# First mixer tile through ScalarE, w_out's loads behind a gating tile and one raw block behind a bank copy, in a two-layer attention and gated-mixer kernel

## The chip, the cores and the metric

The kernel runs on one core of a Trainium2 chip. The metric is the device time of one execution in microseconds (us). Five engines work beside each other, each through its own list of instructions in order: PE (TensorE, matmuls), DVE (VectorE), ACT (ScalarE), POOL (GpSimd) and SP, which here issues every DMA. Semaphores tie them together.

## The reference

Two layers, each an attention block and a gated mixer block, on x of 2048 rows by 640 columns, in float32:

```
x = x + attention(layernorm(x));  x = x + mixer(layernorm(x))      # twice
attention: 32 heads of 20, four segments of 512 rows; in each a softmax of
    q k^T and a memory read phi(q) M / (phi(q) z), mixed by a gate; then @ wo
mixer:  z  = gelu(x @ w_in)                   # 640 -> 1728
        z1 = z[:, :864];  z2 = layernorm(z[:, 864:])
        g  = w_sp @ z2 + b_sp                 # 2048 x 2048 over the rows
        out = (z1 * g) @ w_out                # 864 -> 640
```

## The kernel before

Precision: a float32 operand is split into a float16 high half (a cast on ACT) and a low half (a subtraction on DVE or POOL); three float16 matmuls stand for one product. A split tile is turned by a transposing DMA from SP. A "tile" of rows is 128 of the 2048, so there are 16.

**Attention** (both layers): a hand-written order of PE's work by pairs of heads. The softmax's exponentials P and Pb are written by ACT, which also makes their high half PH (L1257); the low half PL (L1259) is POOL's, but for the last `TAIL` = 2 head pairs' second half, which DVE does. The output projection (yps, L1018) adds to x (xt, L1024) and stores it; the last four tiles' projection is left to the next stage.

**Mixer input** (function `phase1b`, L318 on): for each tile, x is loaded (L330; L333 where the projection is still due), normalised to xn, split into xnhl and transposed to th (`split_t`, L293 to L295). Then 30 matmuls (zp, L375) with each half of w_in: wi1 first (the z2 half, L388), wi0 after it (z1, L411). The first tile's xn is made by POOL (L359), the other tiles' by DVE (L287). xn and xnhl share a place in SBUF with tiles that the last attention step still uses. z2 is cut into blocks zh, zl for phase 2, z1 goes to DRAM. In layer 0 this stage also prepares w_out and the first row pair of w_sp (class `Rows`): the steps of `Rows.first` are tied one by one to the gelus, among them `scales(0)`, the maxima `am` (L464) of the loaded wr tiles and the powers of two from them.

**Phase 2**: eight row pairs p. The 2048 x 2048 product is done by a Strassen-like scheme with seven products of 24 matmuls a pair (L621, banks ga, gb, gc, gd in PSUM), from blocks wt and sums wts of w_sp; the results are copied out of the banks by ACT (u, L688) and added by DVE (L691), gated with z1 (cz loaded at L626, u at L633), split, transposed (ut, L647) and multiplied with w_out (cyp, L657, the "tail"). While pair p is multiplied, pair q = p + 1 is prepared: raw blocks (`raw`: wn on ACT L478 and DVE L479, transposed L484) named "21", "12", "11", "22", each of two ACT instructions, and sums on POOL (ts, L591) with splits (wts) on ACT L598 and DVE L599.

**What sets the order.** For PE, ACT, DVE and POOL it follows the code's order as a tile scheduler puts it, with `issue_after` and priorities as hints. SP's queue is one list; each DMA waits at least for the one eight issues before it, and a DMA that waits holds those behind it. Split weights are kept in DRAM by layer 0 and loaded from there in layer 1 (L107 and L1341).

Of the kernel before, what the change touches and what calls it, by code (L numbers as in the profile page):

```python
# [20 lines left out]
NT = S // 128  # L21
# [63 lines left out]
class Weight:  # L85
# [11 lines left out]

    def load(self, stage, width=864, tag="wst", late=False):
# [19 lines left out]
        for k in range(self.nk):  # L118
            n = 128 if k < full else rest
            for c in range(0, self.cols, width):  # L120
                w = min(width, self.cols - c)
                if late and len(last) == 2:
                    split()
                    yield
                if tag == "wr":
                    if k == 0:
                        both = stage.tile([128, S], F32, tag=tag, name="wst")
                    st = both[:n, 1024 * (k % 2):1024 * (k % 2) + w]
# [112 lines left out]
def other_scales(g, stage, pool, psum, tag):  # L241
# [18 lines left out]
    yield False  # L260
    parts = pow2_parts(g, pool, psum, tag, g.wam, 3, 4)
# [28 lines left out]
def split_t(g, hl, t, src, low=None):  # L290

    nc = g.nc
    nc.scalar.copy(hl[:, 0], src)  # L293
    g.low = (low or nc.vector).tensor_tensor(hl[:, 1], src, hl[:, 0], ALU.subtract)
    nc.sync.dma_start(t.rearrange("p i k c -> p (i k) c"), hl.rearrange("p i c -> p (i c)"), transpose=True)  # L295
# [15 lines left out]
def phase1b(g, o_d, x, x1_d, z1_d, zh, zl):  # L311

    nc, tc = g.nc, g.tc
    with ExitStack() as ctx:
        pool = lambda n, b, **k: ctx.enter_context(tc.tile_pool(name=n, bufs=b, reuse_waits="tile", **k))
        pe2, pe3, pe1 = pool("be2", 2), pool("be3", 3), pool("be1", 1)
        wp0, px1, p2, px2, p3 = pool("bw0", 1), pool("bx1", 1), pool("b2", 1), pool("bx2", 1), pool("b1", 3)
        pz1, py, pz0 = pool("bz1", 2, space=PSUM), pool("by", 1, space=PSUM), pool("bz0", 1, space=PSUM)  # L318
        g.wi[0].tiles(wp0)
# [19 lines left out]
        def attn_out(t, *a):  # L339
# [15 lines left out]
            if t:  # L355
                layernorm(g, x1, xn, D, 2, XS)
            else:
                mv, rs = layernorm_stats(g, x1, D, 2, XS)
                nc.gpsimd.tensor_scalar(xn, x1, mv[:, 0:1], rs, ALU.subtract, ALU.mult)  # L359
            return xn  # L360

        def xn_t(xn):
            th = pe3.tile([128, 2, KD, 128], F16, tag="th", name="th")
            hl = pe1.tile([128, 2, D], F16, tag="xnhl", name="xnhl")
            split_t(g, hl, th, xn)
# [48 lines left out]
        with tc.high_priority(offset=HP2):  # L414
            a = load(0)
            xn = attn_out(0, *a)
            a = load(ORDER[1])
            th = xn_t(xn)
        for i, t in enumerate(ORDER):
# [8 lines left out]
            th1 = xn_t(xn) if i + 1 < NT else None  # L428
# [15 lines left out]
class Rows:  # L444
# [14 lines left out]
    def scales(self, q):  # L459
        g, nc, sc = self.g, self.g.nc, self.g.wsc  # L460
        am = g.small.tile([128, 2, 2], F32, tag="am", name="am")
        for c in range(2):
            for r in range(2):
                nc.vector.tensor_reduce(am[:, r, c:c + 1], self.ws[q, c][:, r], AX.XY, ALU.max, apply_absolute_value=True)  # L464
        pw = sc[:, 0, q]
# [20 lines left out]
    def first(self, pool):  # L486
# [31 lines left out]
        with at():  # L518
            self.scales(q)
# [16 lines left out]
def phase2(g, b_sp, x1_d, z1_d, zh, zl, out):  # L536
# [3 lines left out]
    with ExitStack() as ctx:  # L540
# [83 lines left out]
        def load_z1(t):  # L624
            z1 = p1.tile([128, FH], F32, tag="z1", name="cz1")
            nc.sync.dma_start(z1, z1_d[t])  # L626
# [55 lines left out]
        for p in range(NP):  # L682
# [38 lines left out]
            if q and p:  # L721
                raw(q, "11")

            close = tail(*ready) if p else lambda: None
            copy(A, 1, left)
            if q:
                raw(q, "22")
            if p + 2 < NP:
                e = rows.load(p + 2)
# [25 lines left out]
            z1 = load_z1(p)  # L755
            if q:
# [4 lines left out]
            ready = turn(p + 8, u[1], *held)  # L761
            if q:
# [103 lines left out]
class Attention:  # L866
# [6 lines left out]
    TAIL = 2  # L873
# [60 lines left out]
    def start(self):  # L934

        g, nc = self.g, self.nc
        for t in self.qk:
            for h in range(2):
                r = slice(64 * h + 60, 64 * h + 64)
                with ExitStack() as ctx:  # L940
                    if g.hold:
                        ctx.enter_context(self.tc.issue_after(g.hold[2].ins))
                    nc.sync.dma_start(t[r], g.qc[r])

    def prep(self, t):
# [21 lines left out]
        def last():  # L967
# [3 lines left out]
            split_t(g, hl, self.xt[s % 2][:, :, :, c], xt, low=nc.gpsimd)  # L971
# [594 lines left out]
```

## Time and profile before

| | |
|---|---|
| median of 3 runs | 2297.23 us (2293.0 to 2298.25) |
| profiled execution | 2293.45 us |
| its span | 2291.7 us, mean granted PE clock 0.982 |
| layer 0: mixer input from | 624.08 us |
| layer 1: mixer input from | 1746.72 us |

The profile gives, for one execution, each instruction's start and duration, the idle time of its engine before it with what ended that (in square brackets), the waits of an engine by line, and for a stretch of time the busy time of every engine with PE's granted clock (1.00 is full speed). Numbers of tiles are left out of the names. The line numbers in the profile are those of the code above.

### The profile page before, as it was taken

The numbers are of one execution on the slowest core, as the hardware profiler recorded it, in microseconds if no ns is written. First come the engines' busy times: TensorE is split into PE (matmuls) and PEld (weight loads), VectorE is DVE, ScalarE is ACT, GpSimd is POOL, SyncE is SP. The second block draws the span as 40 slices with busy tenths as digits, with TensorE's granted clock in tenths as the row PEclk, the third lists the DMA queues.
The fourth block names the chain that finished last, engine by engine and source line by source line (L and its number), as shares of the span: only waits on it lengthen the run. The fifth ranks groups of instructions, "written<-read, shape, count | busy, mean of one in ns | idle before, by whom it ended". The sixth has DMA issues, their size and how long they took to land.

```text
span 2291.7 us, 53099 instructions
## 1 busy us (share of the span) xinstructions
PE 2105.1 (92%) x21322; PEld 1267.3 (55%) x21322; DVE 1598.9 (70%) x2761; ACT 1252.4 (55%) x1637; POOL 1459.3 (64%) x1300
## 2 busy tenths in 40 slices
PE   6888888999699999999988999989997999999998
PEld 3454555666455555555554556666664555455555
DVE  7677788777687757878745777787765664566563
ACT  4577788888644433333314888888873333333331
POOL 2377888999745445456512889999995443465560
PEclk9999899999899999999999999999998999999999
DMA  5565657444666787676555347553454346777853
GB/s 166 160 154 151 152 151 191 111 117 127 174 179 179 193 223 184 145 180 177 140 146 127 101 115 181 125 120 94 122 132 132 85 114 200 181 184 172 187 132 81
DMA packets 538616, 342.80 MB, mean 150 GB/s; under 512 B 413536, under 2 KB 463968, under 8 KB 538112
## 3 DMA queue, kind: packets, MB, share of 16 engines
q1 hardware_dynamic: 538368, 339.40, 57.6%
q8 instruction: 167, 2.74, 0.5%
q14 instruction: 81, 0.66, 0.1%
HBM read 159.19 MB, written 92.55 MB: 110 GB/s over the span
## 4 chain that ended last, share of the span: by engine, by line
PE 49%; DVE 19%; POOL 9%; DMA 8%; ACT 7%; issue 5%; SPq 2%; DVEq 0%; ACTq 0%; POOLq 0%
PE zp L375 11%; PE ga L621 8%; POOL PL L1259 6%; PE cyp L657 4%; PE qps L1045 3%; PE gb L621 3%; PE pv L1287 3%; PE vps L986 2%; DVE mxs L1248 2%; PE mp L1184 2%; PE kps L1045 2%; DVE wts L599 2%; PE gc L621 2%; PE gd L621 2%; ACT PH L1257 2%
## 5 line engine op out<-in xcount | busy, mean ns | idle before, releaser
L1259 POOL TENSOR_TENSOR PL<-P,PH 128x640 f16<-128x640 f32 x380 | 534.1, 1430 | 51.8 <-PE pv L1287 40.9
L1248 DVE TENSOR_REDUCE mxs<-mp 128x2 f32<-128x1024 f32 (+2 forms) x384 | 320.4, 862 | 145.7 <-PE mp L1175 144.1
L1222 ACT ACTIVATE P<-es,sc 128x1024 f32<-128x1024 f32 (+1 forms) x256 | 271.5, 1061 | 97.3 <-PE es L1175 87.3
L375 PEld LDWEIGHTS <-th 128*128 128x128 f16 x1920 | 188.8, 99 | 194.7 <-DMA th<-xnhl 28.1
L591 POOL TENSOR_TENSOR ts<-ts,wt 128x512 f32<-128x512 f32 x196 | 267.9, 1378 | 11.0
L1257 ACT CAST PH<-P 128x1280 f16<-128x1280 f32 x192 | 239.7, 1248 | 1.9 <-ACT P L1222 0.4
L621 PEld LDWEIGHTS <-wts 128*128 128x128 f16 x1536 | 151.1, 98 | 151.6 <-issue 24.9
L621 PE MATMUL ga<-zh,wts 128*128 128x432 f16 x768 | 213.1, 349 | 18.8 <-ACT u L688 18.8
L281 POOL TENSOR_TENSOR lnrs<-lnve,mhalf 128x1 f32<-128x1 f32 x96 | 60.1, 635 | 258.2 <-DVE lnve L280 238.3
L1259 POOL TENSOR_TENSOR PL<-Pb,PH 128x640 f16<-128x640 f32 x124 | 176.2, 1446 | 18.0 <-PE pv L1287 15.8
L591 POOL TENSOR_TENSOR ts<-wt,wt 128x512 f32<-128x512 f16 x28 | 37.0, 1320 | 235.3 <-DMA wt<-wn 235.3
L986 PE MATMUL vps<-wvh,xt 128*128 128x320 f16 x640 | 156.7, 312 | 29.1 <-DVE relu L1077 21.4
L375 PE MATMUL zp<-wi1h,th 128*128 128x432 f16 x640 | 152.0, 353 | 25.6 <-DMA th<-xnhl 25.5
L1287 PE MATMUL pv<-vs,PL 128*128 128x41 f16 x2560 | 157.4, 181 | 12.7 <-POOL PL L1259 8.4
L657 PE MATMUL cyp<-wuh,ut 128*128 128x320 f16 (+1 forms) x896 | 163.6, 299 | 4.3 <-DMA ut<-un 3.4
L621 PEld LDWEIGHTS <-wt 128*128 128x128 f16 x1152 | 112.7, 98 | 96.5
L657 PEld LDWEIGHTS <-ut 128*128 128x128 f16 (+1 forms) x1344 | 131.1, 98 | 59.2 <-DMA ut<-un 5.7
L1184 PEld LDWEIGHTS <-qk 64*128 64x128 f16 (+1 forms) x2048 | 78.5, 94 | 153.6 <-issue 134.7
L1287 PE MATMUL pv<-vs,PH 128*128 128x41 f16 x2560 | 160.0, 182 | 2.0 <-DVE ab L1303 2.0
L375 PE MATMUL zp<-wi0h,th 128*128 128x432 f16 x640 | 148.5, 346 | 3.0 <-ACT z L411 3.0
L1287 PEld LDWEIGHTS <-PL 128*128 128x128 f16 x2560 | 140.4, 96 | 14.8 <-POOL PL L1259 10.2
L688 ACT ACTIVATE u<-ga,bsp,wsc 128x432 f32<-128x432 f32 x64 | 45.4, 710 | 186.7 <-PE ga L621 174.9
(218 smaller groups left out, 5455.8 us busy)
## 6 DMA issues: line engine op xcount, KB each, us to landing
qk<-st SPq DMA_DIRECT2D x256, 120.0 KB
wr<-in_B_w_sp_dram SPq DMA_DIRECT2D x60, 512.0 KB
z<-z SPq DMA_DIRECT2D x32, 432.0 KB
cz<-z SPq DMA_DIRECT2D x32, 432.0 KB
xt<-in_A_x_dram SPq DMA_DIRECT2D x32, 320.0 KB
st<-qhl SPq DMA_DIRECT2D x40, 256.0 KB
st<-khl SPq DMA_DIRECT2D x40, 256.0 KB
x<-x SPq DMA_DIRECT2D x32, 320.0 KB
```

The lines of the kernel that those rows point to most:

```text
L375: nc.tensor.matmul(zp[:, n, :FHH], a[:, k, :], b[:, k, c:c + FHH], start=(k == 0 and j == 0), stop=(k == KD - 1 and j == 2))
L591: nc.gpsimd.tensor_tensor(t, a, t if b == "t" else get(b), ALU.add if op == "+" else ALU.subtract)
L621: nc.tensor.matmul(ps, w[:, a, k % 4, :], z[:, k, j, :], start=start and k == 0 and i == 0, stop=k == NP - 1 and i == 2, skip_group_check= ...
L657: nc.tensor.matmul(yp[:, n, :320], a[:kn[k], k, :], b[:kn[k], k, n * 320:(n + 1) * 320], start=(k == 0 and j == 0), stop=(k == KO - 1 and ...
L986: nc.tensor.matmul(ps, a[:, k, c], b[:, k, n * 320:(n + 1) * 320], start=(i == 0), stop=(i == 14))
L1045: nc.tensor.matmul(ps, a[:, k, c], b[:, k, :], start=(i == 0), stop=(i == 14))
L1184: nc.tensor.matmul(out[:, h, o:o + w], a[r, ac], b[r, bc], start=o == 0, stop=False, skip_group_check=True)
L1222: g.exp = nc.scalar.activation(P, E, AF.Exp, scale=g.esc)
L1248: e = nc.vector.tensor_reduce(mx[:, :, n, j], mp[:, :, o:o + w], AX.X, ALU.max)
L1257: nc.scalar.copy(PH, P[:, h])
L1259: (nc.gpsimd if h == 0 or n < self.N - self.TAIL else nc.vector).tensor_tensor(PL[:, c], P[:, h, c], PH[:, c], ALU.subtract)
L1287: nc.tensor.matmul(pv[:, i, h, :], x[:, c:c + 128], v[:, j, h0 + h, :], start=(j == 0 and x is PH), stop=(j == i and x is PL), skip_group_ ...
```

## The change

Eight edits, in the order of the work:

1. In layer 0's attention one of the weight-scale steps comes one step later (`other_scales`).
2. `TAIL` is 1: the low half PL of the last pair but one goes from DVE to POOL.
3. The first mixer tile: DVE makes the negated mean, ACT subtracts the mean (xn) and scales the high half by 1/sigma (xnhl), DVE makes the low half with both in one operation, and SP transposes; POOL has no part but in 1/sigma's power. The pools are opened in another order, so that xn, xnhl, the x tiles and th's first buffer lie over the key weights, which are dead by then.
4. w_in's first half lies in one tile for both its halves, and its loads in layer 0 are staged through four slots (two wr tiles) in place of two.
5. `Rows.scales(0)` is spread over two gelu steps; what follows comes one gelu later.
6. Phase 2, pair 0: z1's tile is loaded ahead of w_out; eight of w_out's fourteen loads stand behind it, the other six behind the next transpose.
7. Phase 2, pairs 1 to 6: the raw block "11" stands behind the copy of bank A.
8. Start of layer 1: the low halves of tiles 2 and 3 are DVE's, and the twelve constant loads (qc) stand behind tile 3's transpose.

Its core:

```diff
-        pe2, pe3, pe1 = pool("be2", 2), pool("be3", 3), pool("be1", 1)
+        pe2, pe1, pe3 = pool("be2", 2), pool("be1", 1), pool("be3", 3)
...
-            else:
-                mv, rs = layernorm_stats(g, x1, D, 2, XS)
-                nc.gpsimd.tensor_scalar(xn, x1, mv[:, 0:1], rs, ALU.subtract, ALU.mult)
-            return xn
+                return xn, None
+            mv, rs = layernorm_stats(g, x1, D, 2, XS)
+            neg = g.small.tile([128, 1], F32, tag="neg", name="neg")
+            nc.vector.tensor_scalar(neg, mv[:, 0:1], -1.0, None, ALU.mult)
+            nc.scalar.activation(xn, x1, AF.Identity, bias=neg)
+            return xn, rs
...
+                nc.scalar.activation(hl[:, 0], xn, AF.Identity, scale=rs)
+                nc.vector.scalar_tensor_tensor(hl[:, 1], xn, rs, hl[:, 0], ALU.mult, ALU.subtract)
+                nc.sync.dma_start(th.rearrange("p i k c -> p (i k) c"), hl.rearrange("p i c -> p (i c)"), transpose=True)
...
-        with at():
-            self.scales(q)
+        parts = self.scale_parts(q)
+        for _ in range(2):
+            with at():
+                next(parts, None)
...
             product(A, p, 2, False)
-            if q and p:
-                raw(q, "11")
...
             copy(A, 1, left)
+            if q and p:
+                raw(q, "11")
...
-            if p == 0:
-                with tc.issue_after(e.ins):
-                    for _ in g.wu.load(None):
-                        pass
...
             z1 = load_z1(p)
+            if p == 0:
+                wu = g.wu.load(None)
+                with tc.issue_after(g.z1.ins):
+                    for _ in range(4):
+                        next(wu)
...
             ready = turn(p + 8, u[1], *held)
+            if p == 0:
+                with tc.issue_after(g.hold[2].ins):
+                    for _ in wu:
+                        pass
...
-    TAIL = 2
+    TAIL = 1
...
-                        ctx.enter_context(self.tc.issue_after(g.hold[2].ins))
+                        ctx.enter_context(self.tc.issue_after(self.fourth.ins))
...
+            e = split_t(g, hl, self.xt[s % 2][:, :, :, c], xt, low=nc.vector if g.hold and t in (2, 3) else nc.gpsimd)
```

Three places in the order of instructions. First SP's queue at the start of layer 1's mixer, before (L295 is tile 0's transpose, L107 loads w_in, L1026 stores x):

```order
L333 DMA xt<-x_0_12 128x640
L1026 DMA x_1_11<-xt 128x640
L107 DMA wi0h<-w_i0h 128x864
L107 DMA wi0l<-w_i0l 128x864
L107 DMA wi0h<-w_i0h 128x864
L107 DMA wi0l<-w_i0l 128x864
L107 DMA wi0h<-w_i0h 128x864
L107 DMA wi0l<-w_i0l 128x864
L107 DMA wi0h<-w_i0h 128x864
L107 DMA wi0l<-w_i0l 128x864
L107 DMA wi0h<-w_i0h 128x864
L107 DMA wi0l<-w_i0l 128x864
```

Tile 0's transpose is the next row, behind all ten. The same place now (L1053 stores x, L377 is tile 0's transpose, L111 loads w_in):

```order
L1053 DMA x_1_10<-xt 128x640
L377 DMA_TRANSPOSE th<-xnhl 128x10x128
L1053 DMA x_1_11<-xt 128x640
L111 DMA wi_27858<-w_i0h 128x864
L111 DMA wi_27858<-w_i0l 128x864
L111 DMA wi_27858<-w_i0h 128x864
L111 DMA wi_27858<-w_i0l 128x864
```

The transpose moved ahead of the ten loads, of a store and of the xt load. In layer 0 it stands between the xt load (L338 now, L333 before) and the store of x_0_11.

Second SP's queue in phase 2's pair 0 of layer 0, before (wuh and wul are w_out, cz is z1's tile, ut the transpose):

```order
L107 DMA wuh<-w_uh 128x640
L107 DMA wul<-w_ul 128x640
L107 DMA wuh<-w_uh 96x640
L107 DMA wul<-w_ul 96x640
L626 DMA cz_13890<-z_0_0 128x864
L647 DMA_TRANSPOSE ut<-un 128x14x128
L626 DMA cz_14146<-z_0_9 128x864
L647 DMA_TRANSPOSE ut<-un 128x14x128
```

And now:

```order
L468 DMA wr<-in_B_w_sp_dram 128x2x512 x4
L646 DMA cz_13878<-z_0_0 128x864
L111 DMA wuh<-w_uh 128x640
L111 DMA wul<-w_ul 128x640
L111 DMA wuh<-w_uh 128x640
L111 DMA wul<-w_ul 128x640
L111 DMA wuh<-w_uh 128x640
```

z1's tile moved from behind fourteen loads of w_out to ahead of them.

Third ACT's list in phase 2, one pair p of layer 0, before (u are the copies of bank A, wn the raw blocks, wts the casts of sums):

```order
L688 ACTIVATE u<-ga,bsp,wsc 128x432
L478 ACTIVATE wn<-wr,wsc 128x512 x6
L688 ACTIVATE u<-ga,bsp,wsc 128x432
L478 ACTIVATE wn<-wr,wsc 128x512 x2
L598 CAST wts_16208<-ts_15816 128x512
```

And now:

```order
L708 ACTIVATE u<-ga,bsp,wsc 128x432
L496 ACTIVATE wn<-wr,wsc 128x512 x4
L708 ACTIVATE u<-ga,bsp,wsc 128x432
L496 ACTIVATE wn<-wr,wsc 128x512 x4
L618 CAST wts_16210<-ts_15818 128x512
```

Two of the eight raw instructions moved behind the second copy.

More of the change, by code (lines that the diff above doesn't have):

```diff
@@ L96, in tiles, with paired @@
         return self.h, self.l
+    def paired(self, pool):
+        t = pool.tile([128, self.nk, 2, self.cols], F16, tag=f"w{self.nm}", name=f"w{self.nm}")
+        self.h, self.l = t[:, :, 0], t[:, :, 1]
     def load(self, stage, width=864, tag="wst", late=False):
@@ L126, in load @@
                     if k == 0:
-                        both = stage.tile([128, S], F32, tag=tag, name="wst")
-                    st = both[:n, 1024 * (k % 2):1024 * (k % 2) + w]
+                        four = [stage.tile([128, S], F32, tag=tag, name="wst") for _ in range(2)]
+                    st = four[k // 2 % 2][:n, 1024 * (k % 2):1024 * (k % 2) + w]
                 else:
@@ L260, in other_scales @@
     yield False
+    yield False
     parts = pow2_parts(g, pool, psum, tag, g.wam, 3, 4)
@@ L294, in split_t @@
     g.low = (low or nc.vector).tensor_tensor(hl[:, 1], src, hl[:, 0], ALU.subtract)
-    nc.sync.dma_start(t.rearrange("p i k c -> p (i k) c"), hl.rearrange("p i c -> p (i c)"), transpose=True)
+    return nc.sync.dma_start(t.rearrange("p i k c -> p (i k) c"), hl.rearrange("p i c -> p (i c)"), transpose=True)
 def split_psum(g, h, l, ps, mult=1.0):
@@ L417, in phase1b @@
             a = load(ORDER[1])
-            th = xn_t(xn)
+            th = xn_t(*xn)
         for i, t in enumerate(ORDER):
@@ L427, in phase1b @@
                 a = load(ORDER[i + 2])
-            th1 = xn_t(xn) if i + 1 < NT else None
+            th1 = xn_t(*xn) if i + 1 < NT else None
             if i > 0:
@@ L459, in scales, with scale_parts @@
     def scales(self, q):
+        for _ in self.scale_parts(q):
+            pass
+    def scale_parts(self, q):
         g, nc, sc = self.g, self.g.nc, self.g.wsc
@@ L464, in scales @@
                 nc.vector.tensor_reduce(am[:, r, c:c + 1], self.ws[q, c][:, r], AX.XY, ALU.max, apply_absolute_value=True)
+            if not c:
+                yield
         pw = sc[:, 0, q]
@@ L720, in phase2 @@
             product(A, p, 2, False)
+            close = tail(*ready) if p else lambda: None
+            copy(A, 1, left)
             if q and p:
                 raw(q, "11")
-            close = tail(*ready) if p else lambda: None
-            copy(A, 1, left)
             if q:
@@ L728, in phase2 @@
             if p + 2 < NP:
-                e = rows.load(p + 2)
-            if p == 0:
-                with tc.issue_after(e.ins):
-                    for _ in g.wu.load(None):
-                        pass
+                rows.load(p + 2)
             if p and q:
@@ L970, in last @@
             hl = self.e2.tile([128, 2, D], F16, tag="xh", name="xnhl")
-            split_t(g, hl, self.xt[s % 2][:, :, :, c], xt, low=nc.gpsimd)
+            e = split_t(g, hl, self.xt[s % 2][:, :, :, c], xt, low=nc.vector if g.hold and t in (2, 3) else nc.gpsimd)
+            if t == 3:
+                self.fourth = e
         return stats, norm
```

11 lines of the change are left out of this document (7 added, 4 removed).

## Prediction

> **What bounds the kernel now.** I read the page first: TensorE (PE) is busy for 92% of the span, so time can only come out of the remaining 8%, or out of matmuls that run at a lower clock. Then the list of waits of PE from 620 us to the end of layer 1 (what it waits for; us in total, times, longest).
>
> ```profile
> PE 2105.1 (92%) x21322; PEld 1267.3 (55%) x21322; DVE 1598.9 (70%) x2761; ACT 1252.4 (55%) x1637; POOL 1459.3 (64%) x1300
> PE zp L375 <- DMA th<-xnhl: 25.5, 6, 11.2
> PE ga L621 <- ACT u L688: 18.8, 10, 4.2
> ```
>
> The mixer's first matmuls (zp) wait 25.5 us for the transposed th, and phase 2's matmuls (ga) wait 18.8 us for an ACT copy (u) that frees their PSUM bank. Those are the places that the change touches, so I read the timeline around each. Layer 0's mixer start, with the queue of SP and the granted clock of the stretch behind it:
>
> ```profile
> 611.57 0.34 SPq L333 DMA_DIRECT2D xt<-in_A_x_dram  x1
> 613.53 2.51 POOL L359 TENSOR_SCALAR xn<-x,lnmv,lnrs 128x640 f32<-128x640 f32 x1 [5.81 <-PE yps L1018]
> ...
> 616.07 0.73 ACT L293 CAST xnhl<-xn 128x640 f16<-128x640 f32 x1 [8.73 <-POOL xn L359]
> 617.71 1.12 DVE L294 TENSOR_TENSOR xnhl<-xn,xnhl 128x640 f16<-128x640 f32 x1
> 618.86 2.28 SPq L295 DMA_TRANSPOSE th<-xnhl  x1
> 624.08 0.90 PE L375 MATMUL zp<-wi1h,th 128*128 128x432 f16 x2 [9.63 <-DMA th<-xnhl]
> ...
> 624.08:629.00 4.92, 4.92 (x14) 2.09 (x15) 1.95 (x2) 3.02 (x3) 0.00 (x0) 0.50 0.91 234
> ```
>
> PE stops at 624.08 - 9.63 = 614.45. POOL can only normalise x at 613.53, because xn lies over a buffer that the last output projection (yps) reads; then the split, the transpose issue at 618.86 and 5.2 us to landing. After the pause, 4.92 us run at clock 0.50: 4.92 x 0.50 = 2.5 us more. Layer 1 repeats it, with ten loads of w_in's half ahead of the transpose in SP's queue:
>
> ```profile
> 1729.78 0.33 SPq L1026 DMA_DIRECT2D x<-xt  x1
> 1734.97 0.43 SPq L107 DMA_DIRECT2D wi0h<-w_i0h  x1
> ...
> 1740.88 1.90 SPq L295 DMA_TRANSPOSE th<-xnhl  x1
> 1746.72 0.90 PE L375 MATMUL zp<-wi1h,th 128*128 128x432 f16 x2 [11.21 <-DMA th<-xnhl]
> 1746.72:1752.00 5.28, 5.28 (x15) 2.24 (x16) 0.83 (x1) 2.01 (x2) 0.00 (x0) 0.50 0.88 225
> ```
>
> The pause is 11.21 us, the half clock 5.28 x 0.50 = 2.6 us. Later in layer 0's mixer there is one more pause of note; the busy times of two stretches of 20 us (PE, PE's weight loads, DVE, ACT, POOL, then clock) and two rows of the timeline:
>
> ```profile
> 640.00:660.00 20.00, 19.16 (x109) 10.31 (x108) 18.62 (x36) 10.80 (x19) 9.77 (x10) 1.00 0.69 162
> ...
> 680.00:700.00 20.00, 16.98 (x99) 9.48 (x97) 15.97 (x28) 6.86 (x11) 9.86 (x10) 1.00 0.90 263
> ...
> 685.04 1.22 DVE L464 TENSOR_REDUCE am<-wr 128x1 f32<-128x1024 f32 x1 [2.47 <-DMA wr<-in_B_w_sp_dram]
> ...
> 695.08 0.53 PE L375 MATMUL zp<-wi0h,th 128*128 128x432 f16 x2 [3.02 <-ACT z L411]
> ```
>
> This pause of 3.02 us leaves the clock of its stretch at 1.00. At full clock a matmul of zp takes 19.16 / 109 = 0.18 us, 30 of them 5.3 us.
>
> The sum below is made against the profiled execution (2293.45 us: span 2291.7 and 1.75 around it). The median of the three runs is 3.78 us above it; I take the same gains off the median.
>
> **Part 1, the first mixer tile (xn, xnhl, th of tile 0).** The change puts xn and xnhl over the key weights, which nothing reads any more by then, and takes POOL out. In return ACT does two activations of 128x640, 0.73 us each by its cast of that size. DVE does a small operation and one like the 1.12 us subtraction. They stand in the last third of the attention, beside PE's work, and ACT is busy for 55% of the span: 0, or 2 us a layer if a score waits behind them. So the transpose is bound by its place in SP's queue alone. *Layer 0:* it stands directly behind the xt load, which waits for the last readers of Pb (611.57 + 0.34 = 611.9). With the 5.2 us from issue to landing of the row above it lands at 617.1, and PE pauses 617.1 - 614.45 = 2.7 us. The pause of 3.02 us above left the clock at 1.00, so I count no half clock. Gain 9.63 + 2.5 - 2.7 = 9.4; bounds 6 (the xt load 3 us later, for its readers' sake) and 12.1 (no pause). *Layer 1:* there it stands behind the store at 1729.78, ahead of the ten loads; it lands by 1730.1 + 5.8 = 1735.9, and PE stops at 1746.72 - 11.21 = 1735.5. That is 0.4 us. What is late next is the tenth load, issued as before near 1741 and wanted in order by the second 30 matmuls, from 1735.9 + 5.3 = 1741.2, and tile 8's transpose behind them; I leave 1 us for these. Gain 11.21 + 2.6 - 1.4 = 12.4; bounds 9 and 13.8.
>
> **Part 2, the low halves of the last head pairs (TAIL).** One pair's PL moves from DVE to POOL in each layer.
>
> ```profile
> 600.81 8.33 DVE L1259 TENSOR_TENSOR PL<-P,PH 128x640 f16<-128x640 f32 x2
> 609.86 1.56 DVE L1259 TENSOR_TENSOR PL<-Pb,PH 128x640 f16<-128x640 f32 x2 [0.25 <-PE pv L1287]
> ...
> 600.94 2.75 POOL L1259 TENSOR_TENSOR PL<-P,PH 128x640 f16<-128x640 f32 x2
> ...
> 608.47 0.19 PE L1287 MATMUL pv<-vs,PL 128*128 128x41 f16 x1 [3.02 <-DVE PL L1259]
> ```
>
> Beside POOL's casts the DVE pair took 8.33 us, and PE waited 3.02 us for it; on POOL it would cost 2.75. But the Pb pair that stays on DVE took 1.56 only because POOL was through by then; POOL's row of casts is now 2.75 longer, and if the two overlap, Pb may take what the P pair took, 6.8 us more. I take 0, between a gain of 3 and a loss of 4 a layer, since the row that goes and the row that threatens are of one kind. The Trainium skill ("SBUF — State Buffer", on the two separate sides) says that a DVE operation with two SBUF inputs and a GpSimd operation exclude each other for whole instructions. By turns the pair would take 2 x (0.78 + 1.38) = 4.3 us; this trace's 8.33 is beyond that, so the rows decide.
>
> **Part 3, inside layer 0's mixer.** The weight scales take two steps in place of one. DVE stands 2.47 us for a load in front of the maxima (am), and PE stops 3.02 us for what follows. With half the maxima a step later, DVE passes on. But DVE is busy 18.62 of 20 us a little earlier, and everything is one gelu later: I take 1 (0 to 3). One scale step later in layer 0's attention, wi's paired tile and the four staging slots move small operations in stages where PE runs on; their cover is PE's work there; 0, or 1 us each way if the cover goes.
>
> **Part 4, phase 2's first pair.** SP issues four loads of w_sp (wr) until 852.0, then fourteen of w_out, and only then z1's tile (cz), which the gate's product u waits for:
>
> ```profile
> 849.47 2.55 SPq L456 DMA_DIRECT2D wr<-in_B_w_sp_dram  x4
> ...
> 863.60 0.37 SPq L626 DMA_DIRECT2D cz<-z  x1
> 868.58 1.56 DVE L633 TENSOR_TENSOR u<-u,cz 128x864 f32<-128x864 f32 x1 [3.96 <-DMA cz<-z]
> ...
> 875.09 0.52 PE L621 MATMUL ga<-zh,wts 128*128 128x432 f16 x1 [3.53 <-ACT u L688]
> 875.09:879.00 3.91, 3.91 (x13) 1.71 (x13) 3.91 (x5) 0.00 (x0) 0.00 (x0) 0.58 0.61 117
> 1984.32 1.06 DVE L633 TENSOR_TENSOR u<-u,cz 128x864 f32<-128x864 f32 x1 [4.70 <-DMA cz<-z]
> ...
> 1990.34 0.34 PE L621 MATMUL ga<-zh,wts 128*128 128x432 f16 x1 [4.15 <-ACT u L688]
> ```
>
> Behind the wr loads, cz issues near 852 and has until 868.58 - 3.96 = 864.6, when DVE is free. That is 12 us for a transfer that took 868.5 - 863.6 = 4.9, with the four wr loads ahead of it. DVE starts 3.96 us earlier, which covers the 3.53 us of PE, and the half clock's 3.91 x 0.42 = 1.6 goes with it: 5.2. Layer 1: 4.15 and a like 1.6, covered by 4.70 of DVE: 5.6, taking off 0.2. The six w_out loads that now stand behind the ut transpose issue in 6 x (863.60 - 852.0) / 14 = 5 us, until some 870, and are first read by the w_out tail behind those 24 ga matmuls, which end about 5 us after 871.6. Bounds 2 and 5.8 each: cz may still come late behind wr.
>
> **Part 5, the third raw block behind the bank copy, pairs 1 to 6.** ACT copies bank A (u) behind six raw halves (wn), of which the fifth waits for a transpose. The wait list of 880 to 1125 and ACT's rows in pair 1; then pair 3 of layer 1:
>
> ```profile
> PE ga L621 <- ACT u L688: 9.5, 6, 1.7
> 885.88 0.72 ACT L478 ACTIVATE wn<-wr,wsc 128x512 f16<-128x512 f32 x1 [2.34 <-DMA wt<-wn]
> ...
> 887.91 0.69 ACT L688 ACTIVATE u<-ga,bsp,wsc 128x432 f32<-128x432 f32 x1
> ...
> 2077.44 0.72 ACT L478 ACTIVATE wn<-wr,wsc 128x512 f16<-128x512 f32 x1 [2.29 <-DMA wt<-wn]
> ...
> 2080.75 0.71 ACT L688 ACTIVATE u<-ga,bsp,wsc 128x432 f32<-128x432 f32 x1 [1.21 <-PE ga L621]
> ...
> 2083.08 1.45 POOL L591 TENSOR_TENSOR ts<-wt,wt 128x512 f32<-128x512 f16 x1 [15.28 <-DMA wt<-wn]
> ```
>
> In layer 0 u would start with the fourth wn's end, 885.88 - 2.34 = 883.5, in place of 887.91; the six waits (9.5 us) go. The wn behind it starts at 885.88 as before, since the transpose sets it. I take 8 of 9.5: PE then runs closer on the later sums, whose slack no row shows; bounds 4 and 9.5. In layer 1 u waits for PE until 2080.75 and the raw halves queue behind it: they come some 3.3 us later (2080.75 against 2077.44), and so may POOL's sums. No wait of PE stands there now, so that cost is 0 unless the slack is under 3.3 (rival D).
>
> **Part 6, between the layers.** Twelve constant loads (qc) stand ahead of tile 2's transpose:
>
> ```profile
> 1181.87 9.97 SPq L943 DMA_DIRECT2D qk<-qc  x12
> ...
> 1187.16 2.76 POOL L294 TENSOR_TENSOR xnhl<-xt,xnhl 128x640 f16<-128x640 f32 x2 [0.80 <-ACT xnhl L293]
> 1192.38 3.07 SPq L295 DMA_TRANSPOSE xt<-xnhl  x2
> ...
> 1196.02 0.45 PE L986 MATMUL vps<-wvh,xt 128*128 128x320 f16 x1 [4.16 <-DMA xt<-xnhl]
> ```
>
> Without them the transpose goes with the split's end, 1188 to 1189.9 (DVE's 1.12 against POOL's 1.38 apiece), at least 2.5 us sooner, and two transposes are no longer issued in one go. 4.16 is at stake, and 1.6 if a half clock follows it as after the 3.53; I leave 1.2 for the key weights' load that still fills the queues: 4.6, bounds 2 and 5.8. The qc loads are wanted only by the scores, after all of vps.
>
> **The sum.** 9.4 + 12.4 + 0 + 1 + 5.2 + 5.6 + 8 + 4.6 = 46.2 us: 2297.2 - 46.2 = 2251.0 (2247.2 on the profiled execution's scale). About 0.2%, 4.6 us, is what a measurement of this kernel can tell from none.
>
> **The rivals.**
> *A, given back in the mixer (0.15).* DVE at 18.62 of 20 us becomes the bound of layer 0's mixer once it starts earlier, so that part 1's 9.4 comes back as waits before 700: 2260. For it: DVE's row; against: in that same stretch PE lost only 0.84 us.
> *B, phase 2 keeps its wait (0.12).* cz lands late behind the wr loads, and pairs 1 to 6 meet the next late sum: 5.2 + 5.6 + 4 are lost: 2266.
> *C, the change does not do what it says (0.05).* The transposes stand earlier in SP's queue but issue no earlier, because the queue itself stands, as for 9.97 us at the twelve qc loads: 9.4 + 12.4 are lost: 2273.
> *R, the port rule on TAIL (0.10).* DVE's Pb pair runs beside POOL's longer row and takes 8.33 in place of 1.56; less the 3.02 us of PE that go, that is 3.8 us later at each layer's end: 2251 + 7.6 = 2259. For it: the 8.33; against: POOL's casts took 2.75 beside it, so the overlap may be short. The Trainium skill's page named in part 2 has the rule by which the two exclude each other.
> *D, slower (0.04).* The raw block behind the copy makes every later sum late. Price: 3.3 us and the 2.29 wait inside it, 5.6 in each of 12 pairs, 67 us, and part 5's 8 is not had: 2251 + 75 = 2326. It decides from the point where the slack in layer 1 is under 3.3 us, and wins over the gains when it is under some 1.5.
>
> **How the numbers follow.** The forecast has 0.54, with its own range 2243 to 2259 (its terms' bounds do not all fall to one side). A, R and B lie up to 2266. The range 2240 to 2270 leaves out C, D and the forecast's far ends. Faster by over 0.2%: all but D and a heap of small losses, 0.93; same 0.03; slower 0.04.
>
> **What would show it.** Right: zp's first wait under 4 us in layer 0 and under 2 in layer 1, both at clock near 1.0; no wait of ga on u in pair 1; ga's waits on u in pairs 1 to 6 gone; vps on xt under 1.5. Wrong: new waits of ga or gb on wts in layer 1's pairs (D), waits of zp on z before 700 (A), pv waiting for DVE's PL (R).

## The result and the profile after

The changed kernel takes 2277.91 us (median of 4 runs, 2274.11 to 2279.61) against 2295.11 us (4 runs, 2291.43 to 2298.25) for the kernel before on the same chip: a ratio of 0.9923, with a 95% interval of 0.9901 to 0.9945. That is a gain of some 17 us where 46 were forecast. The profiled executions (2279.19 and 2293.45 us) differ by 14.3 us. The page of the changed kernel shows PE as the busiest engine still, and no other engine near it:

```profile
PE 2107.4 (93%) x21322; PEld 1266.8 (56%) x21322; DVE 1606.0 (71%) x2761; ACT 1250.7 (55%) x1639; POOL 1458.3 (64%) x1300
```

So a loss must stand in waits of PE or in its clock. The first step is a ledger: the same matmul is looked up in both traces at each seam between the stages, and the distances are compared. In the table pv is the attention's last matmul, zp the mixer's first, gb and gd the first of those banks in phase 2's pairs 0 and 7, cyp the last of w_out's tail; us from one to the next.

| stretch | before | after | change | forecast |
|---|---|---|---|---|
| layer 0: start to last pv | 614.3 | 618.2 | +4.0 | 0 |
| last pv to first zp | 9.8 | 2.0 | -7.8 | -6.9 |
| first zp to gb of pair 0 | 225.4 | 236.3 | **+10.8** | -3.5 |
| gb of pair 0 to gd of pair 7 | 285.7 | 272.3 | -13.4 | -13.2 |
| gd of pair 7 to last cyp | 47.2 | 53.7 | **+6.5** | 0 |
| layer 1: last cyp to last pv | 552.9 | 554.2 | +1.3 | -4.6 |
| last pv to first zp | 11.4 | 0.0 | -11.4 | -10.8 |
| first zp to gb of pair 0 | 217.4 | 218.7 | +1.2 | -1.6 |
| gb of pair 0 to gd of pair 7 | 276.0 | 270.9 | -5.1 | -5.6 |
| gd of pair 7 to the end | 51.6 | 51.2 | -0.4 | 0 |

The four large gains came as forecast, within 1 us each (-37.7 against -36.5 in sum). The losses are in stretches that the forecast held to be neutral or better, above all the two in bold. The list of PE's waits from 0 to 2290 us (what it waits for; us in total, times, longest) names what is new there:

```profile
PE ga L641 <- ACT u L708: 11.2, 9, 3.8
...
PE yps L1045 <- DVE xt L1051: 8.5, 2, 5.4
PE zp L387 <- DMA th<-xnhl: 7.6, 7, 2.0
PE zp L387 <- ACT z L423: 5.7, 1, 5.7
...
PE gc L641 <- DMA wt<-w: 2.8, 1, 2.8
```

The wait for th fell from 25.5 to 7.6 us and that for u from 18.8 to 11.2. But yps waits 8.5 us for DVE's residual sum xt, and gc 2.8 us for a transfer; neither wait was there before. Each is followed to its cause in the timeline.

**The end of layer 0's attention** (DVE, POOL, PE and SP from 603 to 621 us):

```profile
603.35 2.75 POOL L1286 TENSOR_TENSOR PL<-P,PH 128x640 f16<-128x640 f32 x2
603.40 9.77 DVE L292 TENSOR_SCALAR xn<-x,lnmv,lnrs 128x640 f32<-128x640 f32 x1 [0.32 <-POOL lnrs L286]
...
606.94 2.75 POOL L1286 TENSOR_TENSOR PL<-P,PH 128x640 f16<-128x640 f32 x2
609.65 2.75 POOL L1286 TENSOR_TENSOR PL<-Pb,PH 128x640 f16<-128x640 f32 x2
612.35 0.47 POOL L1334 TENSOR_TENSOR gm<-ab 128x160 f32<-128x160 f32 x1
613.09 0.54 DVE L1051 SCALAR_TENSOR_TENSOR xt<-yps,sc,xt 128x320 f32<-128x320 f32 x1
613.68 0.42 PE L1045 MATMUL yps<-woh,o 128*128 128x320 f16 x1 [3.08 <-DVE xt L1051]
620.22 0.54 PE L387 MATMUL zp<-wi1h,th 128*128 128x432 f16 x1 [1.81 <-DMA th<-xnhl]
```

Tile 8 is the mixer's second. Its normalisation (xn, L292) writes one of the tiles that the change put over the key weights, so it no longer waits for the attention's buffers and DVE takes it early, among the attention's own work. There it stands for 9.77 us, until 613.17, 0.35 us after the last operation of POOL's row, and the residual sum xt queues behind it. In the kernel before it came only after the attention:

```profile
618.87 0.64 DVE L287 TENSOR_SCALAR xn<-x,lnmv,lnrs 128x640 f32<-128x640 f32 x1
```

How long such an operation takes otherwise in the changed kernel, the group of that line shows (count; shortest, median and longest in ns):

```profile
L292 DVE TENSOR_SCALAR xn<-x,lnmv,lnrs x30: 606/612/10396, 603.4 to 1909.9; 128x640 f32<-128x640 f32 x30
```

The median is 0.61 us; the 10396 is the same instruction in layer 1. There PE's yps waits 5.45 us:

```profile
1716.96 10.40 DVE L292 TENSOR_SCALAR xn<-x,lnmv,lnrs 128x640 f32<-128x640 f32 x1 [1.69 <-POOL lnrs L286]
...
1727.87 0.42 PE L1045 MATMUL yps<-woh,o 128*128 128x320 f16 x1 [5.45 <-DVE xt L1051]
```

What these waits cost on balance is less than their length in layer 0, since another wait went from the same place: the 3.02 us of pv for DVE's PL. Set side by side matmul by matmul, the last pv comes 3.96 us later than before, but 2.39 us of that are already there at the pv that ran at 599.0 us before (now at 601.4). The end of layer 0's attention thus costs 1.6 us. In layer 1 the same reckoning, from the pv at 1708.0 us on, gives 4.2 us.

**Layer 0's mixer.** The pause of zp near 690 us has grown from 3.02 to 5.67 us, and phase 2 now starts with a wait of gc. The matmul after the pause, then SP's issue of the first row pair's blocks and the matmul that waits for them:

```profile
693.58 0.52 PE L387 MATMUL zp<-wi,th 128*128 128x432 f16 x1 [5.67 <-ACT z L423]
...
815.62 4.37 SPq L599 DMA_DIRECT2D wt<-w  x6
...
823.08 0.36 PE L641 MATMUL gc<-zh,wt 128*128 128x432 f16 x1 [2.85 <-DMA wt<-w]
```

Half-speed stretches follow some of the pauses (window, its length, then busy us of PE, its weight loads, DVE, ACT and POOL; granted clock, DMA share, GB/s): behind layer 0's first zp, the wait of ga near 845, layer 1's first zp (where the clock is full), the last row pair of layer 0 (told below) and the long pause. In the trace's clock records the clock is either 0.50 or 1.00; a value between them is a window that holds some of both.

```profile
620.22:624.00 3.78, 3.78 (x12) 1.69 (x13) 3.78 (x4) 3.20 (x5) 1.56 (x2) 0.55 0.42 120
845.08:849.00 3.92, 3.92 (x13) 1.68 (x13) 2.00 (x3) 1.17 (x2) 0.00 (x0) 0.56 0.35 66
1736.75:1740.70 3.95, 3.95 (x28) 2.15 (x25) 1.60 (x4) 0.72 (x1) 1.76 (x3) 1.00 0.78 253
1137.16:1142.43 5.27, 5.27 (x15) 2.17 (x15) 0.65 (x2) 0.00 (x0) 0.00 (x0) 0.50 0.01 3
693.58:698.69 5.11, 5.11 (x15) 2.19 (x15) 4.86 (x6) 2.12 (x4) 3.20 (x3) 0.50 0.73 227
```

The excess of the third stretch of the ledger is then made up of +2.65 (the longer pause), +2.6 (5.11 x 0.50 behind it), +2.85 (gc), +3.2 (ga: 4.0 us in two waits in place of 0.8 in one) and +1.7 (3.92 x 0.44 behind the longer of them), less 1.7 (later waits for th: 3.0 in place of 4.7) and 0.8 (the first zp's half clock, 3.78 x 0.45 = 1.7 in place of 2.5): 10.5 of the 10.8.

**The last row pair of layer 0**, ACT and PE (before, the same three rows stood at 1137.78, 1138.30 and 1139.60 with no such wait in the list):

```profile
1135.88 0.62 ACT L618 CAST wts<-ts 128x512 f16<-128x512 f32 x1 [2.51 <-POOL ts L611]
1136.41 0.70 ACT L708 ACTIVATE u<-ga,bsp,wsc 128x432 f32<-128x432 f32 x1
1137.16 0.52 PE L641 MATMUL ga<-zh,wts 128*128 128x432 f16 x1 [3.79 <-ACT u L708]
```

PE comes to this pair 6.4 us earlier than before, the chain from POOL's sum through ACT's cast to the bank copy u only 1.9 us earlier (1136.41 against 1138.30). PE waits 3.79 us, and 5.27 us at clock 0.50 cost 2.6 more: together the whole lead of 6.4 us.

These traces suggest three causes: **S**, the extra gelu step fetches phase 2's first row pair too late; **L**, in layer 0's last pair ACT's cast of the fourth sum (s4) stands ahead of the bank copy; **X**, tile 8's xn stands beside POOL's row. The rivals: DVE is the bound of layer 0's mixer and gives the gains back there (A of the prediction); and **T**, that w_in's four staging slots pack its splits ahead of tile 8's and delay the early mixer.

### The profile page after: what moved, and what is told of

Read it like the earlier page. It is cut to its first block, busy times and chain, and to the rows that moved or that the text cites. A ratio compares the mean times of both kernels' runs of the same rounds, so it can differ in the third digit from the quotient of the medians.

```text
span 2277.5 us, 53085 instructions
## 1 busy us (share of the span) xinstructions
PE 2107.4 (93%) x21322; PEld 1266.8 (56%) x21322; DVE 1606.0 (71%) x2761; ACT 1250.7 (55%) x1639; POOL 1458.3 (64%) x1300
## 4 chain that ended last, share of the span: by engine, by line
PE 48%; DVE 16%; POOL 10%; DMA 9%; ACT 8%; issue 6%; SPq 2%; ACTq 0%; DVEq 0%; POOLq 0%
PE zp L387 9%; PE ga L641 9%; POOL PL L1286 6%; PE cyp L677 5%; PE qps L1072 3%; PE pv L1314 3%; PE vps L1013 3%; PE mp L1211 2%; PE kps L1072 2%; PE gb L641 2%; DVE mxs L1275 2%; PE gc L641 2%; ACT PH L1284 2%; PE gd L641 2%; PE es L1211 1%
## 5 line engine op out<-in xcount | busy, mean ns | idle before, releaser
L387 PEld LDWEIGHTS <-th 128*128 128x128 f16 x1920 | 188.1, 98 | 179.7 <-DMA th<-xnhl 11.4
L611 POOL TENSOR_TENSOR ts<-ts,wt 128x512 f32<-128x512 f32 x196 | 280.1, 1440 | 11.1 <-DMA wt<-wn 0.2
L641 PE MATMUL ga<-zh,wts 128*128 128x432 f16 x768 | 214.1, 351 | 11.3 <-ACT u L708 11.2
L387 PE MATMUL zp<-wi,th 128*128 128x432 f16 x960 | 183.7, 350 | 5.7 <-ACT z L423 5.7
L1211 PE MATMUL es<-qk 64*128 64x512 f16 (+3 forms) x1024 | 124.8, 300 | 24.6 <-ACT P L1249 20.0
L1314 PEld LDWEIGHTS <-PL 128*128 128x128 f16 x2560 | 140.7, 97 | 11.5 <-POOL PL L1286 11.4
```

Source lines behind the costliest of these rows:

```text
L387: nc.tensor.matmul(zp[:, n, :FHH], a[:, k, :], b[:, k, c:c + FHH], start=(k == 0 and j == 0), stop=(k == KD - 1 and j == 2))
L611: nc.gpsimd.tensor_tensor(t, a, t if b == "t" else get(b), ALU.add if op == "+" else ALU.subtract)
L641: nc.tensor.matmul(ps, w[:, a, k % 4, :], z[:, k, j, :], start=start and k == 0 and i == 0, stop=k == NP - 1 and i == 2, skip_group_check= ...
L1211: nc.tensor.matmul(out[:, h, o:o + w], a[r, ac], b[r, bc], start=o == 0, stop=False, skip_group_check=True)
L1314: nc.tensor.matmul(pv[:, i, h, :], x[:, c:c + 128], v[:, j, h0 + h, :], start=(j == 0 and x is PH), stop=(j == i and x is PL), skip_group_ ...
```

## The experiments

Ten runs follow, on three chips. Each ratio holds against runs of the kernel before on the same chip (medians 2289.67, 2294.21 and 2292.8 us). The changed kernel was run again on the second chip alone (ratio 0.9917 [0.99, 0.9933]), so a ratio from the first or third is set beside the changed kernel's only through the kernel before. A stretch of the ledger is named by its two ends, as in the table above.

### The scales in one step again (S)

```diff
-        parts = self.scale_parts(q)
-        for _ in range(2):
-            with at():
-                next(parts, None)
+        with at():
+            self.scales(q)
```

> The changed kernel with the weight scales of layer 0's mixer in one step again. Theory S (the fourteenth step puts the last loads of the first row pair one gelu later, and that is what makes phase 2 of layer 0 start late): the wait of gc for the block wt (2.85 us) and the wait of ga for the bias load (3.2 us, with 1.7 us of half clock behind it) go; phase 2's first pair starts some 6 to 8 us earlier, and the pause of zp near 693 (5.67 us) stays within 2 us of itself. Theory D (DVE and the loads of w_sp bound that stage whatever the steps): the pause near 693 stays or grows and phase 2's first pair starts within 2 us of where it does now. Time against the changed kernel: S 5 to 8 us less, D within 2 us.

Measured: 2269.55 us, ratio 0.9905 [0.9878, 0.9932]. PE's waits from 815 to 850 us, of the changed kernel and of this one:

```profile
PE ga L641 <- ACT u L708: 3.2, 1, 3.2
PE gc L641 <- DMA wt<-w: 2.8, 1, 2.8
```

```profile
PE ga L639 <- ACT u L706: 1.4, 2, 0.8
```

The wait of gc is gone with the step, so S holds: the step delayed the fetch of the first blocks by one gelu and PE stood for it. From the first zp to pair 0's gb this run takes 228.7 us, where the changed kernel took 236.3 (232.8 in a second execution) and the kernel before 225.4. In the total the gain of 5 to 8 us that was expected is not shown, since the interval overlaps the changed kernel's. The pause near 690 only fell to 4.90 us, so the step is not its main cause.

### The last pair's cast behind the bank copy (L)

```diff
-                if not q:
-                    split(p, "s4")
...
-            if p and q:
+            if p:
                 split(p, "s4")
```

> The changed kernel with the last pair's split of s4 behind the copy of bank A, as in the pairs before it. Theory L (layer 0's last pair pays back what the pairs before gained, because the copy of bank A stands behind casts of POOL's last sum): the wait of ga on u near 1137 (3.79 us) and the half clock behind it (3.84 us at 0.50) go, 5 to 6 us less, and layer 1's phase 2 stays as it is. Rival (POOL's sums are late as such, and the wait only moves to the next product that reads s4): the wait reappears as one of ga on wts some 9 us later, under 2 us less.

Measured: 2268.57 us, ratio 0.9904 [0.9883, 0.9925]. PE's waits from 870 to 1150 us, which in the changed kernel hold the one of 3.8 us:

```profile
PE ga L641 <- ACT u L708: 1.9, 4, 0.8
```

The longest is 0.8 us, and no wait of ga stands later in the pair either. From gd of pair 7 to the last cyp this run takes 47.1 us, against 53.7 in the changed kernel and 47.2 before: L holds, and the 6.5 us are shown at their place. In the total they are not, since the intervals overlap.

### Tile 8 centred on ACT too (X)

Tile 8's xn goes the way of the first tile, over ACT, and so out of DVE's queue.

```diff
-            if t:
+            if t and t != ORDER[1]:
                 layernorm(g, x1, xn, D, 2, XS)
```

> The changed kernel with tile 8, the second of the mixer, centred and scaled on ACT like the first. Theory B (DVE's normalisation of tile 8, which now comes early, took 9.8 and 10.4 us because it can't run while POOL's casts follow one another, and the residual sum xt behind it kept the projection waiting): the waits of yps on xt of 3.08 us (layer 0) and 5.45 us (layer 1) go; 6 to 8 us less if they are not eaten by the stage behind, of which layer 1's 4 to 5 should stay in the total and layer 0's may be eaten. Rival (PL casts left on DVE are the cause): the waits stay within 1 us, no change in the total.

Measured: 2270.1 us, ratio 0.9915 [0.9889, 0.9941]. The waits of yps on xt are gone in both layers. PE's waits from 600 to 620 us show what is late next:

```profile
PE pv L1314 <- DVE ab L1330: 2.9, 1, 2.9
...
PE zp L387 <- DMA th<-xnhl: 1.8, 1, 1.8
```

The same row of 2.9 us stands in layer 1. So DVE's xn did hold xt back, but in layer 0 3.08 us of wait turned into 2.9 of another, and in layer 1 5.45 into 2.9. Matched matmul by matmul as above, the ends of the two attentions now cost 0.3 and 1.9 us against the kernel before, in place of 1.6 and 4.2. The total cannot be told from the changed kernel's.

### TAIL back at 2, the control for X

If DVE's xn waits out POOL's row, it must get shorter by exactly what is taken out of that row: the two PL operations of one pair, 2.75 us.

```diff
-    TAIL = 1
+    TAIL = 2
```

> The changed kernel with TAIL 2: the last pair but one's second low half on DVE again. Theory B (POOL's unbroken row of casts blocks DVE's normalisation): POOL's row is two casts shorter, but DVE gets its pair of 5 to 8 us back; the waits at the end of both attentions stay between 2 and 6 us a layer; total within 4 us. Rival (moving the pair to POOL is what made DVE late): the waits of yps on xt fall under 1 us in both layers and the total falls by 4 to 8 us.

Measured: 2276.36 us, ratio 0.9936 [0.9913, 0.9959]: no gain over the changed kernel. DVE's two rows, layer 0 and layer 1:

```profile
601.09 7.06 DVE L292 TENSOR_SCALAR xn<-x,lnmv,lnrs 128x640 f32<-128x640 f32 x1 [0.32 <-POOL lnrs L286]
...
1714.16 7.69 DVE L292 TENSOR_SCALAR xn<-x,lnmv,lnrs 128x640 f32<-128x640 f32 x1 [1.69 <-POOL lnrs L286]
```

9.77 - 7.06 and 10.40 - 7.69 are both 2.71 us: the row's two operations of PL. Here too xn ends 0.35 us after the last operation of POOL's row. Its time is POOL's row and not its own work. That is shown; the price in total is not. In layer 0 the wait of yps is gone, but pv waits 3.4 us for DVE's PL, and in layer 1 yps still waits 2.7 us and zp again 3.9 us for th.

### The changed kernel once more

> The changed kernel itself once more, on the chip of the three runs beside it, to have them compared on one chip. All theories: the ratio against the kernel before between 0.990 and 0.9945, as measured.

Measured: 2272.55 us, ratio 0.9917 [0.99, 0.9933], a gain of 21.7 us on this chip. Its profiled execution tells which of the new waits belong to the kernel. The first zp and PE's waits from 815 to 850 us:

```profile
618.14:622.10 3.96, 3.96 (x22) 2.16 (x23) 3.96 (x4) 3.81 (x5) 1.66 (x3) 1.00 0.38 110
```

```profile
PE gc L641 <- DMA wt<-w: 3.5, 1, 3.5
PE ga L641 <- ACT u L708: 1.3, 2, 0.8
```

The waits of yps (3.1 and 5.4), gc (3.5), the last pair (3.62) and the pause near 690 (5.87) are all there again. The wait of 3.2 us of ga near 845 and the half clock at the first zp (its pause was 1.2 us here and not 1.81) are not. Pair 0's gb comes at 850.94, 232.8 us after the first zp in place of 236.3, so 3.5 of the 10.8 us come and go between executions (the wait of ga near 845 stands in X's run again, 3.1 us long). Matched as above, the ends of the two attentions cost 2.2 and 4.2 us here, while at 599 us only 0.3 us had been lost, not 2.39.

### The kernel before with the raw block moved (part 5 alone)

```diff
             product(A, p, 2, False)
-            if q and p:
-                raw(q, "11")
 
             close = tail(*ready) if p else lambda: None
             copy(A, 1, left)
+            if q and p:
+                raw(q, "11")
```

> The kernel before with one part of the change alone: raw block 11 behind the copy of bank A. Theory L: the six waits of ga on u in pairs 1 to 6 of layer 0 (9.5 us) shrink to under 2, but the last pair, whose s4 cast stands ahead of its bank copy, pays 3 to 6 us of it back as one wait of ga on u near 1130 (with half clock); net gain 3 to 6 us; layer 1 unchanged within 1 us. Rival D of the prediction (the later raw block makes POOL's sums late in every pair): waits of ga or gb on wts in layer 1's pairs, no gain or a loss.

Measured (10 runs): 2289.88 us, ratio 0.9982 [0.9968, 0.9997], that is 0.7 to 7.3 us. PE's waits from 880 to 1160 us:

```profile
PE ga L621 <- ACT u L688: 5.4, 4, 3.7
```

The six waits of 9.5 us of the kernel before have become four of 5.4, of which 3.7 us is one wait, at 1134.5 in the last pair: the numbers of the changed kernel (5.4, 4 times, longest 3.8). In layer 1's pairs PE's list is empty, so rival D's late sums did not come. Part 5 alone gains 9.5 - 1.7 = 7.8 us in pairs 1 to 6, as forecast, and in the same breath makes the last pair's wait of 3.7 us: from gd of pair 7 to the last cyp this run takes 53.7 us, as the changed kernel does.

### Two staging slots again (T)

```diff
-                        four = [stage.tile([128, S], F32, tag=tag, name="wst") for _ in range(2)]
-                    st = four[k // 2 % 2][:n, 1024 * (k % 2):1024 * (k % 2) + w]
+                        both = stage.tile([128, S], F32, tag=tag, name="wst")
+                    st = both[:n, 1024 * (k % 2):1024 * (k % 2) + w]
```

> The changed kernel with w_in's first half staged through two slots again, as before. Theory T (layer 0's mixer does not use its earlier start because the second tile's transpose is no earlier: ACT and DVE split four pieces of w_in, 3.7 and 4.8 us, ahead of tile 8's split): the second tile's transpose issues 2 us or more earlier against the first, the gelus of the z2 half from the second on come 2 to 4 us earlier against the start of zp, and phase 2 of layer 0 starts 2 to 4 us earlier. Rival (the stage is held by DVE's work and the w_sp loads further on): the second gelu may move, but the pause of zp near 690 grows by as much and phase 2 starts within 1 us of where it does.

Measured (5 runs): 2278.72 us, ratio 0.9937 [0.9914, 0.9961]. ACT's rows show the opposite of T:

```profile
629.90 1.01 ACT L81 ACTIVATE wi<-wst,iv 128x864 f16<-128x864 f32 x1 [1.84 <-DMA wst<-in_B_w_in_dram]
...
632.23 0.98 ACT L400 ACTIVATE z<-zp,sc 128x864 f32<-128x864 f32 x1
```

With two slots each split of w_in waits for its load, and the first gelu (z) comes behind the last of them at 632.23. With four it came seven microseconds earlier in the second execution of the changed kernel, whose first zp started at nearly the same time (618.14 against 617.84):

```profile
625.15 0.98 ACT L400 ACTIVATE z<-zp,sc 128x864 f32<-128x864 f32 x1
```

T falls. From the first zp to pair 0's gb this run takes 240.2 us, more than either execution of the changed kernel; its total cannot be told from theirs.

### S, L and X undone together

The edits of the first three experiments in one kernel.

> The changed kernel with three repairs together: scales in one step, the last pair's s4 behind the bank copy, tile 8 on ACT. If the three waits are independent, as I take them: 7 (phase 2's start) + 6 (last pair) + 7 (both attentions' ends, part of it paid back in layer 1) = 18 to 22 us under the changed kernel on the same chip, ratio to the kernel before about 0.984. If they hide one another: under 12 us.

Measured: 2260.58 us, ratio 0.986 [0.9845, 0.9875], 12 us under the changed kernel on the same chip: a gain that is shown, and less than the 18 to 22 us expected. The last pair's stretch is 47.1 us again. At the end of the attentions the next waits come up: pv's 2.9 us for ab in each layer, and in layer 0 a pause of 2.1 us at the first zp, with half clock behind it. By the trace's clock records that half clock begins at 610.29, behind pv's wait and before zp's:

```profile
612.94:616.90 3.96, 3.96 (x12) 1.66 (x13) 3.96 (x5) 3.21 (x5) 1.65 (x2) 0.50 0.38 116
```

### The pause near 690, one step fewer for w_out

The maxima wait for the second pair of wr loads of w_sp, and these cannot be issued before the last split of w_out frees their buffer. SP's issue of them in the kernel before and in the changed one:

```profile
679.98 1.21 SPq L456 DMA_DIRECT2D wr<-in_B_w_sp_dram  x2
```

```profile
678.72 1.22 SPq L468 DMA_DIRECT2D wr<-in_B_w_sp_dram  x2
```

They come 1.3 us earlier, where PE begins the mixer 3.9 us earlier (620.22 against 624.08): the difference, 2.6 us, is what the pause grew by (5.67 - 3.02). That last split, of w_out's last 96 rows, is a gelu step of its own. Here it shares the step before, with all else as changed.

```diff
-            with at() if k % 2 == 0 else ExitStack():
+            with at() if k in (0, 2, 4) else ExitStack():
```

> The changed kernel with w_out's last split (96 rows) taken into the step before it, so that thirteen steps remain with the scales in two. Theory P (the pause of zp near 690 in layer 0's mixer comes from w_sp's second pair of loads, which can issue only once that last split has freed its buffer, and from the maxima that DVE does in order behind the landing): the second pair issues some 11 us earlier, DVE no longer stands for it, and the pause of 5.7 to 5.9 us falls under 2, with its half clock; with one step less, gc's wait for wt (2.9 to 3.5 us) goes as well: 6 to 10 us less than the changed kernel, ratio to the kernel before about 0.988. Rival (DVE's work bounds that stage): the pause stays above 4 us, and only the wait of gc goes, 3 to 5 us less.

Measured: 2270.05 us, ratio 0.9898 [0.9869, 0.9927]. The last of those loads issues ten microseconds earlier (6.5, counted from the first zp), and PE's waits from 640 to 700 us are spread:

```profile
668.54 0.62 SPq L468 DMA_DIRECT2D wr<-in_B_w_sp_dram  x1
```

```profile
PE zp L387 <- DMA th<-xnhl: 3.8, 2, 3.1
PE yp L353 <- DVE x L356: 1.8, 1, 1.8
```

The wait on z goes with the late load, so that load set it; but 5.6 us of waiting stand at two other places, of th and x, and half clock follows the first of them. What sets these two is open. The wait of gc goes too, since everything behind comes one gelu earlier: the merged step and the scales' extra step stand in the same list. The total is not shown to be less than the changed kernel's.

### All four edits

> The three repairs and the merged step together, the scales in one step. Theory P: the pause near 690 falls under 2 us here too, 4 to 6 us under the three repairs alone, ratio to the kernel before about 0.984. Rival: within 2 us of the three repairs alone (0.986).

Measured: 2257.35 us, ratio 0.9846 [0.9825, 0.9868]. That beats both kernels; against the three edits (0.986 [0.9845, 0.9875]) the intervals overlap, so the fourth edit's own gain is not shown in the total. From the first zp to pair 0's gb this run takes 223.2 us, the only one with a shorter stretch than the kernel before (225.4); the wait on z is 1.1 us there.

## Why the prediction was wrong, step by step

Mechanism and place were right for most of the gains; the sum was wrong because three steps held a moved piece of work to be free.

- **Part 1, the two pauses: right in their sizes, in layer 0 with some luck.** zp's first wait is 1.81 us (forecast 2.7) in layer 0, and 0.03 us between the last pv and zp in layer 1 (0.4), there at clock 1.00. As forecast, the transpose issues right behind the xt load (615.99). But the tile landed at 620.2 and not at 617.1, and PE stopped at 618.40 and not at 614.45: both ends were late by about as much.
- **Part 1, the cover: the step that failed first.** The prediction costed the operations of the first tile alone ("beside PE's work there, 0 or 2 us"). It did not follow the second tile, whose xn lies in the same place. A buffer that comes free early lets every later user of it start early, and this one was put in DVE's in-order queue ahead of the residual sum: 9.77 and 10.40 us in place of 0.61, and waits of 3.08 and 5.45 us of PE that are in no term. On balance with the waits that went, the ends of the two attentions cost 1.6 and 4.2 us (2.2 and 4.2 in the second execution), where the forecast had 0.
- **Part 1, no half clock counted: held in one execution, failed in another.** After 1.81 us the clock was 0.55 for 3.78 us, after 1.2 us it was 1.00. The term rested on one row, a pause of 3.02 us that had left it at 1.00. The same trace had a counterexample in a row that the prediction shows for part 2: pv's pause of 3.02 us at 608.47 had half clock behind it, from 608.70 to 612.11.
- **Part 2 (rival R): a sum of 0, with the wrong instruction held.** pv's wait of 3.02 us for DVE's PL went, as part 2 had it, and yps's 3.08 took its place. DVE was held beside POOL's longer row, but the instruction in the way was tile 8's xn; in layer 0 the Pb pair took 1.54 us (1.56 before), since it starts only when the row has ended. The Trainium skill ("SBUF — State Buffer", the section on who interferes with whom) lists tensor_scalar among the operations that can take the port pair shared with GpSimd, and says that the loser of the lock stands fully blocked; this trace agrees with the blocking. The same section of the Trainium skill gives the lock for the length of an instruction; here 0.61 us of work waited for nine in a row.
- **Part 3: wrong in sign, the second step that failed.** "Everything is one gelu later" was seen and costed at 0 to 3 us of gain. One gelu later also meant the fetch for phase 2's start: gc waits 2.85 us (3.5 in the second execution), shown by undoing the step. And the pause that it was meant for grew by 2.65 us and now has 5.11 us at half clock behind it (4.90 us, and half clock too, with the step undone). What sets that pause is the wr load, which moved 1.3 us forward where PE moved 3.9. So rival A was right that part of the start's gain comes back before 700, and wrong on the cause of that wait: not DVE's load but one transfer tied to a gelu step. For the waits on th and x that took its place with the step merged, DVE's load is not excluded.
- **Part 4 and part 5: right** in the pairs they name: -13.4 us against 13.2 from pair 0 to pair 7 in layer 0, -5.1 against 5.6 in layer 1. The waits of ga on u from 880 us to the last pair fell from 9.5 us in six to this row, where 8 were forecast to go:

```profile
PE ga L641 <- ACT u L708: 1.6, 3, 0.8
```

- **Part 5, behind its pairs: the third step that failed.** "PE then runs closer on the later sums, whose slack no row shows" was costed at 1.5 us and stopped at pair 6. In the last pair no next one is prepared and the cast of s4 stands ahead of the copy. The two traces bound the slack: POOL's and ACT's chain there does not keep step with PE, so what PE gains on it beyond the slack turns into a wait. PE gained 6.4 us, the chain 1.9, and 3.79 us of wait and 2.6 of half clock were paid.
- **Part 6: right at its place** (vps waits 0.6 us for xt in place of 4.16), and then lost in the same stretch, 4.2 us of it at the attention's end.
- **Rivals B, C, D** did not happen: u had its z1 tile in time, the transposes issued early, and no wait of ga or gb stands in layer 1's pairs with the raw block moved alone.

In sum, of the 46.2 us some 32 were not had in the profiled execution: 10.8 + 3.5 in layer 0's mixer, 6.5 in the last pair, 4.0 and 5.9 in the two attentions, 2.8 at layer 1's mixer start, less 1.6 that came above the forecast elsewhere. Of the 9.9 us in the attentions 1.6 and 4.2 arise at their ends. The rest was lost earlier in them, in amounts that differ between the two executions (2.4 and 0.3 us in layer 0, 2.4 and 1.3 in layer 1, less the 0.6 by which part 6's gain there was above its forecast), and its cause is open. The 2.8 us at layer 1's mixer start, with three short waits for th (2.9 us in place of the 1 us left for them), were tried by no run.

## What to carry to other kernels

When buffers are moved so that one operation can start early, list every later instruction that writes the same place: each of them may start early too, and in an in-order queue it stands ahead of work that is wanted sooner. A step added to a list that is tied to another engine's work delays all that follows on the list, so look at the last entry, not the one beside the edit. After a wait is removed, compare the lead that the waiting engine gains with the lead that its suppliers gain, up to the last round of the loop, where the order of preparation differs.

## What the runs showed of the hardware

A DVE operation of 0.61 us stood for 9.77 and 10.40 us beside an unbroken row of POOL operations and was not let in between two of them; with two operations fewer in the row it stood 2.71 us less in both layers.

The half clock does not follow the length of a pause alone: at layer 0's first zp a pause of 1.2 us left 1.00 and one of 1.81 us brought half clock, and in the kernel before a pause of 3.02 us was followed by half clock at 608 us and by 1.00 near 690. The clock records of the twelve traces show more. In each trace every stretch of half clock begins on one fixed grid of 3.41 us and lasts one, two, three or five of its steps (but for the last one, which runs past the end). So the price of half clock comes in units of 1.7 us of PE's work, and what counts first is how busy PE was in the step before (by the matmuls' ends, which are modelled), not the pause as such. Between 60 and 2240 us, a step at full clock in which PE was busy for under 40% was followed by half clock in all 112 cases, one with over 70% in none of 6877, and one between in 57 of 440. Three steps from that middle band (PE's busy time comes behind the length): before, near 690, with full clock behind it; the changed kernel ahead of the first zp, with half clock behind it; and its second execution there, with full clock:

```profile
690.61:694.02 3.41, 1.45 (x11) 0.91 (x10) 2.81 (x8) 0.88 (x2) 2.17 (x3) 1.00 1.09 327
616.77:620.19 3.42, 1.63 (x45) 1.37 (x42) 2.12 (x5) 1.75 (x2) 1.14 (x4) 1.00 1.05 276
616.23:619.64 3.41, 2.21 (x35) 1.43 (x33) 2.58 (x6) 2.66 (x3) 1.50 (x2) 1.00 0.69 178
```

The first was busy for less than the second and kept the clock all the same; what decides within the band is open.
